# On-chip copy for half of KB, no ET transfers, shorter wa and kb loads, and Lu loaded in two parts

## The chip, the cores and the metric

The kernel runs on one core of a Trainium2 chip. The metric is device time: microseconds (us) from the start to the end of one execution. The profiler's record of one execution has a span (first to last instruction) that is a little shorter than that execution's own time.

## The reference

Three layers follow one another. The first is a recurrence over 768 time steps for 4 batches and 8 heads, 32 independent states of 40x40. Its output goes through a mixture of 8 experts with two chosen per token, and that through a dense feed-forward layer.

```python
def _attn_ref(r, k, v, w, a, b):
    state = np.zeros((B, H, D, D))
    for t in range(S):
        y[:, :, t] = np.einsum('bhd,bhde->bhe', rt, state)
        Sa = np.einsum('bhde,bhe->bhd', state, at)
        state_decay = state * wt[:, :, None, :] - np.einsum('bhd,bhe->bhde', Sa, bt)
        state = state_decay + np.einsum('bhd,bhe->bhde', vt, kt)
    return y
...
x = moe(x)                     # top 2 of 8 experts, relu(x @ w1[e]) @ w2[e]
h = x @ w_in
out = (h * tanh(softplus(h))) @ w_out
```

The change touches the recurrence alone, which is the class `Rec` of the kernel.

## The kernel before

The time steps are cut into 24 chunks of 32, and the 32 states into two halves of 16, so that the recurrence is a chain of 48 steps g: chunk g//2, half g%2. Inside a chunk the dependence between time steps is a triangular system of 32x32 for each state; it is solved for groups of 4 chunks at once on VectorE. Three generators run ahead of the chain and are interleaved with it by due times (`pump`): `prepare` (one chunk at a time), `solve` (one group of 4 chunks) and `apply` (one chunk).

`prepare` for a chunk i: VectorE scans the decays w (tile `wa`) to products `E` and reciprocals `R`; GpSimd multiplies `a` by `E` (`abd`, L235) and `k`, `b` by `R` (tile `kb`, L238); TensorE multiplies `abd` and `kb` (`pp`, L283), whose halves go to `Ls`, stored to the scratch `lscr` (L289), and into the tile `AM` (a part of `share`); TensorE transposes `kb` (L301), ScalarE copies it to `kn` (L307), and SyncE stores `kn` to a scratch `knd` in DRAM (L309); the transposed `E` becomes `EN` (L318). The first 40 columns of `AM` are `a` times `EN` (`scale_a`, L269): for that, SyncE loads `AT` and, by a second and a third transfer, moves the two halves of `EN` into the tile `ET`, because `EN` holds two chunks on its 128 partitions and `AM` one.

`solve` loads the four chunks' `lscr` into `Lu` (L411, 128 rows), works on VectorE (L439 to L454) and stores the result `Tt` to `tscr` (L488). `apply` loads `tscr` into the block-diagonal `Tbd` by four transfers (L386) and multiplies it with `AM` (L403) into `Zt`.

The chain at step g: `s_mm` (L561) multiplies the tile `KB` with the state `ST`, and VectorE scales that to the state two steps on (L566); `tr` transposes the state, `u_mm(g + 1)` (L548) gives the next step's rows, `y_mm(g - 1)` (L523) the output, with the right half of `KB` and `RR`; `rv_mm` (L593) fills `RR`. `KB[i % 2]` holds for chunk i, on partitions 64 to 127, the matrix `kn` twice, once for `s_mm` (x = 0) and once for `y_mm` (x = 1). One transfer from `knd` writes both (L496, a read that repeats each row), in the middle of every even step for the chunk after. It can't be issued until `y_mm` of the chunk before the present one has read the tile.

Every DMA named here is issued by SyncE in the order of the program, and each issue waits for what it needs before the next one is looked at. The DMAs take the completion counters DMAHW0 to DMAHW7 in turn, and an issue also waits for the DMA that had its counter before, the eighth one back.

Of the kernel before, what the change touches and what calls it, by code (L numbers as in the profile page):

```python
# [21 lines left out]
C = 32  # L22
NP = 2
# [9 lines left out]
LA = 2  # L33


def layout_rec(inp):

    c = np.ascontiguousarray

    def heads_t(x):  # L40
        return x.reshape(NP, PR, 2, NC, C, D).transpose(3, 2, 5, 1, 0, 4)


    wa = np.zeros((NC, 2, 64, NW + 1 + 2 * PR * C), np.float32)
    w33 = np.ones((NC, 2, 64, PR, 2, C + 1), np.float32)
    w33[..., 0] = 0
    w33[:, :, :D, :, :, 1:] = heads_t(inp["w"])
    wa[..., :NW] = w33.reshape(NC, 2, 64, NW)
    wa[:, :, :D, NW + 1:] = heads_t(inp["a"]).reshape(NC, 2, D, -1)
    at = inp["a"].reshape(NP, PR, 2, NC, C, D).transpose(3, 2, 0, 4, 1, 5)  # L50
    kb = np.zeros((NC, 2, 64, PR, 2, 2, C), np.float32)
    for x, n in enumerate("kb"):
        kb[:, :, :D, :, :, x] = heads_t(inp[n])
    rt = inp["r"].reshape(NP, HH, NC, C, D).transpose(2, 4, 0, 1, 3)
    vn = np.zeros((NC, NP, C, HH, 64), np.float32)
    vn[..., :D] = inp["v"].reshape(NP, HH, NC, C, D).transpose(2, 0, 3, 1, 4)
# [8 lines left out]
class Rec:  # L65


    def __init__(self, ctx, nc, tc, ins, emit_x, ident, share, late):
# [5 lines left out]
        self.pet = P("ret", 1)  # L74
# [9 lines left out]
        self.at = {}  # L84
# [5 lines left out]
    def consts_a(self):  # L90
# [110 lines left out]
    def pair(self, out, x, i, rows=RW):  # L201
        self.nc.sync.dma_start(out=out[0:rows], in_=self.ins[x][i, 0:rows])
# [48 lines left out]
    def load_at(self, i):  # L251

        t = self.last_x if i == 1 else [self.px.tile([128, HH // 2, D], F32, name="X") for _ in range(2)] if i == 2 else [
            self.pet.tile([128, PR, D], F32, name=n) for n in ("AT", "ET")]
        self.nc.sync.dma_start(out=t[0], in_=self.ins["at"][i].rearrange("p (a x) -> p a x", x=D))
        self.at[i] = t

    def load_et(self, i):

        en, et = self.EN[i // 2], self.at[i][1]  # L260
        r = 64 * (i % 2)
        for ab in range(2):
            self.nc.sync.dma_start(out=et[64 * ab:64 * ab + 64], in_=en[r:r + 64, ab])

    def scale_a(self, i):
        self.ready = i + 1
        if i in self.at:
            at, et = self.at.pop(i)
            self.nc.gpsimd.tensor_tensor(out=self.AM[i % (2 * GJ)][:, :, 0:D], in0=at, in1=et, op=ALU.mult)  # L269
# [55 lines left out]
    def prepare(self):  # L325
# [3 lines left out]
        for i in range(GJ, n):  # L329
            pos = iter([i / GJ - 2 + s / (6 * GJ) if i >= 2 * GJ else self.early(start[i - GJ][s]) for s in range(6)])  # L330
            if i == GJ:
# [24 lines left out]
            if i - LA >= GJ:  # L356
                self.scale_a(i - LA)
# [4 lines left out]
            if i == GJ:  # L362
                for x in range(2, GJ):
                    self.load_et(x)
                    self.scale_a(x)
            if i - LA + 1 >= GJ:
                self.load_at(i - LA + 1)
                self.load_et(i - LA + 1)
        for i in range(n - LA, n):
            yield (i + LA) / GJ - 2  # L370
            self.scale_a(i)
            if i + 1 < n:
                yield (i + LA + .5) / GJ - 2
                self.load_at(i + 1)
                self.load_et(i + 1)
# [230 lines left out]
    def chain(self, g, fill):  # L606
        if g == 0:
            self.u_mm(0)
        if g < NG - 2:
# [6 lines left out]
            if g % NP and OPT['kb'] == 1 and g > 1:  # L616
                self.load_kb(g // NP + 1)
# [12 lines left out]
        if g + 2 < NG:  # L630
# [6 lines left out]
            if g % NP == 0 and g and OPT['kb'] == 0:  # L637
                self.load_kb(g // NP + 1)
# [9 lines left out]
    def begin(self):  # L648
# [39 lines left out]
        for i in range(1, 3):  # L688
            self.load_at(i)
# [1049 lines left out]
```

## Time and profile before

| | us |
|---|---|
| median of 3 runs (1428.04 to 1430.09) | 1428.05 |
| profiled execution, own time | 1428.0 |
| its span | 1426.2 |
| busy in the span: PE | 1190.7 |
| DVE | 861.2 |
| ACT | 664.0 |
| POOL | 623.1 |

The profile names the engines PE (TensorE), DVE (VectorE), ACT (ScalarE), POOL (GpSimd) and SP (SyncE, which only issues DMAs here). The recurrence fills about the first 600 us. The first 124 us of it prepare the first chunks; there PE is busy a third of the time. In the rest PE is busy about four fifths of the time, at a mean granted clock of about 0.85 of full speed. The experts and the feed-forward layer fill the rest, where PE is nearly always busy. The chain of waits that ended last leads from the last instruction back through the feed-forward layer on PE and does not reach the recurrence, so that stage is read from its own waits.

### The profile page before, as it was taken

To read this page: it belongs to the slowest core of one execution; us is meant where nothing else is said; L and a number is where in the kernel's file an instruction comes from. 1 tells how busy PE (TensorE), PEld (TensorE's weight loads), DVE (VectorE), ACT (ScalarE), POOL (GpSimd) and SP (SyncE) were. 2 spreads that over 40 slices of the span, in tenths; PEclk is the share of its full clock that TensorE was granted. 3 is DMA by queue.
4 is the path that set the end of the run, shared out by engine and by line. 5 is a ranking of instruction groups with operands and counts; after the bars stand their busy time and mean duration, and the time that the engine had idled before them with its cause. 6 is when DMAs were issued, how large, how long until landed. Compare 5 with 4: busy or idle time off the path is not lost. (4 is left out here: it accounts for less than half of the span.)

```text
span 1426.2 us, 33947 instructions
## 1 busy us (share of the span) xinstructions
PE 1190.7 (83%) x13902; PEld 1135.5 (80%) x13902; DVE 861.2 (60%) x1570; ACT 664.0 (47%) x1419; POOL 623.1 (44%) x556
## 2 busy tenths in 40 slices
PE   3425778878787886885999999999888999999998
PEld 2325767767686775775999999998888999999998
DVE  8475837667493733362867876775236665556653
ACT  3423535545444433531443442442237666676664
POOL 4553734645262524162334544443045554454431
PEclk9557878988878888897999999999989999999999
DMA  6644667667755764424435545644245111110000
GB/s 152 156 132 129 162 152 193 177 149 182 178 132 114 127 111 85 141 77 133 128 104 179 163 148 179 204 142 148 66 114 155 29 36 32 29 47 10 15 15 20
DMA packets 147308, 165.64 MB, mean 116 GB/s; under 512 B 70294, under 2 KB 118422, under 8 KB 147126
## 3 DMA queue, kind: packets, MB, share of 16 engines
q1 hardware_dynamic: 136438, 140.85, 37.8%
q0 software_dynamic: 10688, 22.32, 5.8%
q8 instruction: 120, 1.97, 0.6%
q14 instruction: 62, 0.51, 0.1%
HBM read 116.06 MB, written 43.12 MB: 112 GB/s over the span
## 5 line engine op out<-in xcount | busy, mean ns | idle before, releaser
L1611 POOL TENSOR_TENSOR gl<-fh,gh 128x1024 fp32r<-128x1024 f32 x46 | 131.0, 2878 | 105.2 <-ACT gh L1627 101.9
L1253 PE MATMUL ph<-xh,w1h 128*128 128x256 f32 (+1 forms) x576 | 163.3, 296 | 12.0 <-issue 6.7
L1253 PE MATMUL ph<-xl,w1h 128*128 128x256 f32 (+1 forms) x576 | 162.5, 295 | 0.2
L1579 PE MATMUL fps<-fxh,ih 128*128 128x256 f32 x576 | 156.2, 286 | 1.4 <-DVE fh L1581 1.4
L1579 PE MATMUL fps<-fxl,ih 128*128 128x256 f32 x576 | 153.8, 281 | 0.5 <-DVE fxl L1109 0.3
L1610 DVE TENSOR_TENSOR fh<-fh,fp 128x1024 f32<-128x1024 f32 x48 | 95.0, 2014 | 60.3 <-ACT fp L1609 56.6
L1273 PE MATMUL py<-w2h,hh 128*128 128x320 f32 x400 | 129.2, 323 | 2.4 <-ACT hh L1105 1.6
L1107 DVE SCALAR_TENSOR_TENSOR hl<-ph,hh 128x512 fp32r<-128x512 f32 (+1 forms) x104 | 69.0, 665 | 103.0 <-ACT hh L1105 87.4
L1273 PE MATMUL py<-w2h,hl 128*128 128x320 f32 x400 | 125.7, 314 | 3.8 <-DVE hl L1107 3.6
L1273 PE MATMUL py<-w2l,hh 128*128 128x320 f32 x400 | 125.3, 313 | 2.0 <-DVE w2l L1109 2.0
L1253 PEld LDWEIGHTS ph<-xh,w1h 128*128 128x128 f32 x576 | 114.1, 198 | 13.3 <-issue 9.2
L1253 PEld LDWEIGHTS ph<-xl,w1h 128*128 128x128 f32 x576 | 114.3, 198 | 0.6 <-DVE xl L1109 0.6
L1641 PE MATMUL fpy<-oh,gl 128*128 128x320 f32 x384 | 114.6, 310 | 0.0
L1641 PE MATMUL fpy<-oh,gh 128*128 128x320 f32 x384 | 114.3, 310 | 0.0
L1641 PE MATMUL fpy<-ol,gh 128*128 128x320 f32 x384 | 113.9, 308 | 0.0
L1253 PE MATMUL ph<-xh,w1l 128*128 128x256 f32 (+1 forms) x384 | 112.9, 294 | 0.0
L1581 DVE COPY fh<-fps 128x512 f32<-128x512 f32 x96 | 64.6, 689 | 79.6 <-ACT fp L1580 73.7
L1579 PEld LDWEIGHTS fps<-fxh,ih 128*128 128x128 f32 x576 | 108.9, 189 | 1.8 <-DVE fh L1581 1.7
L1579 PEld LDWEIGHTS fps<-fxl,ih 128*128 128x128 f32 x576 | 109.0, 189 | 1.1 <-DVE fxl L1109 1.1
L1579 PE MATMUL fps<-fxh,il 128*128 128x256 f32 x384 | 107.7, 281 | 0.0
L1105 ACT ACTIVATE hh<-ph 128x512 fp32r<-128x512 f32 (+1 forms) x104 | 59.7, 580 | 98.7 <-PE ph L1253 91.8
L235 POOL TENSOR_TENSOR abd<-wa,E 40x512 f32<-40x512 f32 x40 | 64.4, 1609 | 66.7 <-issue 28.6
(276 smaller groups left out, 3306.4 us busy)
## 6 DMA issues: line engine op xcount, KB each, us to landing
KB<-knd SPq DMA_DIRECT2D x24, 640.0 KB
share<-in_w_dram SPq DMA_DIRECT2D x8, 1280.0 KB
wa<-in_wa_dram SPq DMA_DIRECT2D x22, 422.9 KB
kb<-in_kb_dram SPq DMA_DIRECT2D x20, 416.0 KB
share<-in_w_dram SPq DMA_DIRECT2D x8, 1024.0 KB
knd<-kn SPq DMA_DIRECT2D x24, 320.0 KB
yb<-y SPq DMA_DIRECT2D x22, 320.0 KB
ST<-in_vn_dram SPq DMA_DIRECT2D x48, 128.0 KB
```

Source lines behind the costliest of these rows:

```text
L235: (nc.vector if i <= OPT['nd'] else nc.gpsimd).tensor_tensor(out=abd[r, :, :, ab], in0=a[r], in1=E[r, :, :, 0:C], op=ALU.mult)
L1105: nc.scalar.activation(out=hi, in_=src, func=AF.Relu if relu else AF.Copy)
L1107: nc.vector.scalar_tensor_tensor(out=lo, in0=src, scalar=0.0, in1=hi.bitcast(F32), op0=ALU.max, op1=ALU.subtract)
L1253: nc.tensor.matmul(ph[:, m % c], lhsT=a, rhs=b, start=(q == 0), stop=(q == len(ops) - 1))
L1273: nc.tensor.matmul(py, lhsT=a[:, m, ts], rhs=b[:, m], start=(m == 0 and q == 0), stop=(m == FC - 1 and q == 2))
L1579: nc.tensor.matmul(ph[:, i], lhsT=a, rhs=b, start=(q == 0), stop=(q == len(ops) - 1))
L1581: nc.vector.tensor_copy(h[:, 2 * m2:2 * m2 + 2], ph)
L1610: mul = lambda s: nc.vector.tensor_tensor(out=h[:, s], in0=h[:, s], in1=p[:, s], op=ALU.mult)
L1611: low = lambda s: (nc.vector if last and s.start % 8 else nc.gpsimd).tensor_tensor(out=gl[:, s], in0=h[:, s], in1=gh[:, s].bitcast(F32), o ...
L1641: nc.tensor.matmul(py, lhsT=a[:, m, ts], rhs=w[:, m], start=(q == 0), stop=(q == len(ops) - 1))
```

## The change

`KB`: the transfer from `knd` writes the x = 0 half alone (320 KB in place of 640 KB), and a new `copy_kb` on ScalarE copies it, one step's part at a time, to the x = 1 half, behind the state copies of `u_mm`. The load is issued in odd steps, behind `u_mm`, for two chunks on. It waits for `s_mm` and `copy_kb` of the same step.

`ET`: the tile and its two transfers per chunk are gone. `AT` has one fixed tile, whose partitions 0 to 63 and 64 to 127 take even and odd chunks like `EN`, and `scale_a` multiplies `AT` and `EN` by two operations on 64 partitions, which write across to `AM`. It stands at the end of each chunk's `prepare`, no longer two chunks later, and issues the `AT` load of two chunks on.

Padding: from chunk 4 on, `wa` and `kb` are loaded by two transfers of 40 rows each, without the 24 rows between.

`Lu`: loaded in two parts, 96 rows for the first three chunks of the group, and 32 rows for the last.

```diff
-    at = inp["a"].reshape(NP, PR, 2, NC, C, D).transpose(3, 2, 0, 4, 1, 5)
+    at = inp["a"].reshape(NP, PR, 2, NC, C, D).transpose(3, 0, 4, 2, 1, 5)
...
     def pair(self, out, x, i, rows=RW):
-        self.nc.sync.dma_start(out=out[0:rows], in_=self.ins[x][i, 0:rows])
+
+        for r in (slice(0, rows),) if i < GJ else (slice(0, D), slice(64, RW)):
+            self.nc.sync.dma_start(out=out[r], in_=self.ins[x][i, r])
...
     def load_at(self, i):
-        t = self.last_x if i == 1 else [...] if i == 2 else [
-            self.pet.tile([128, PR, D], F32, name=n) for n in ("AT", "ET")]
-        self.nc.sync.dma_start(out=t[0], in_=self.ins["at"][i].rearrange("p (a x) -> p a x", x=D))
-        self.at[i] = t
-
-    def load_et(self, i):
-
-        en, et = self.EN[i // 2], self.at[i][1]
-        r = 64 * (i % 2)
+        if i < len(self.seq):
+            r = 64 * (i % 2)
+            self.nc.sync.dma_start(out=self.AT[r:r + 64].rearrange("p b a x -> p (b a x)"), in_=self.ins["at"][i])
+
+    def scale_a(self, i):
+
+        self.ready = i + 1
+        en, r = self.EN[i // 2], slice(64 * (i % 2), 64 * (i % 2) + 64)
         for ab in range(2):
-            self.nc.sync.dma_start(out=et[64 * ab:64 * ab + 64], in_=en[r:r + 64, ab])
-
-    def scale_a(self, i):
-        self.ready = i + 1
-        if i in self.at:
-            at, et = self.at.pop(i)
-            self.nc.gpsimd.tensor_tensor(out=self.AM[i % (2 * GJ)][:, :, 0:D], in0=at, in1=et, op=ALU.mult)
+            self.nc.gpsimd.tensor_tensor(out=self.AM[i % (2 * GJ)][64 * ab:64 * ab + 64, :, 0:D], in0=self.AT[r, ab], in1=en[r, ab], op=ALU.mult)
+        self.load_at(i + 2)
...
-    def load_l(self, k):
-        self.nc.sync.dma_start(out=self.Lu[:, 0:C * C], in_=self.lscr[k].rearrange("u q t i -> (u q) (t i)"))
+    def load_l(self, k, j0=0, j1=GJ):
+        self.nc.sync.dma_start(out=self.Lu[32 * j0:32 * j1, 0:C * C],
+                               in_=self.lscr[k][PR * j0:PR * j1].rearrange("u q t i -> (u q) (t i)"))
...
         if k:
+
+            self.wants[1] = lambda: self.made < GJ * (k + 1) - 1
+            yield s0 - .2
+            self.load_l(k, 0, GJ - 1)
             self.wants[1] = lambda: self.made < GJ * (k + 1)
             yield s0 - OPT["ll"]
-            self.load_l(k)
+            self.load_l(k, GJ - 1)
...
     def load_kb(self, i):
+
         KB, kn = self.KB[i % 2], self.KN.pop(i)
-        self.nc.sync.dma_start(out=KB.rearrange("p c x h d -> p x (c h d)")[64:128], in_=kn[:, None].to_broadcast([64, 2, 2 * HH * D]))
+        self.nc.sync.dma_start(out=KB[64:128, :, 0].rearrange("p c h d -> p c (h d)"), in_=kn.rearrange("p (c x) -> p c x", c=2))
+
+    def copy_kb(self, g):
+        t = self.KB[(g // NP) % 2][64:128, g % NP]
+        self.nc.scalar.copy(out=t[:, 1], in_=t[:, 0])
...
         if g + 1 < NG:
             self.u_mm(g + 1)
+        self.copy_kb(g)
+        if g % NP and g // NP + 2 < NC:
+            self.load_kb(g // NP + 2)
...
-            if g % NP == 0 and g and OPT['kb'] == 0:
-                self.load_kb(g // NP + 1)
```

On SyncE, in the middle of the recurrence, one chunk's transfers behind its `knd` stand so before (the names in brackets are what an issue waits for; a counter DMAHWn stands for the DMA that used it last):

```order
L496 DMA KB_140<-knd 64x2x1280 [waits DMAHW5_49,PE_49]
L309 DMA knd<-kn 2x64x640 [waits DMAHW6_49,Activation_49]
L501 DMA ST_422<-in_vn_dram 32x1024 [waits DMAHW7_49]
L506 DMA RR_424<-in_rt_dram 40x1024 [waits DMAHW0_49]
L386 DMA Tbd_190<-tscr 32x8x32 [waits DMAHW1_49]
L386 DMA Tbd_190<-tscr 32x8x32 [waits DMAHW2_49]
L386 DMA Tbd_190<-tscr 32x8x32 [waits DMAHW3_49]
L386 DMA Tbd_190<-tscr 32x8x32 [waits DMAHW4_49]
L255 DMA AT<-in_at_dram 128x320 [waits DMAHW5_49,Pool_49]
L263 DMA ET<-EN 64x320 [waits DMAHW6_49]
L263 DMA ET<-EN 64x320 [waits DMAHW7_49]
```

The `KB` load stood just ahead of `knd`, and the first `ET` was the one that waited for `knd`'s counter, DMAHW6. The same place of the changed kernel, on SyncE, from `knd` on:

```order
L303 DMA knd<-kn 2x64x640 [waits DMAHW5_49,Activation_49]
L486 DMA ST_422<-in_vn_dram 32x1024 [waits DMAHW6_49,PE_49]
L491 DMA RR_424<-in_rt_dram 40x1024 [waits DMAHW7_49,PE_49]
L361 DMA Tbd_188<-tscr 32x8x32 [waits DMAHW0_49]
L361 DMA Tbd_188<-tscr 32x8x32 [waits DMAHW1_49]
L361 DMA Tbd_188<-tscr 32x8x32 [waits DMAHW2_49]
L361 DMA Tbd_188<-tscr 32x8x32 [waits DMAHW3_49]
L255 DMA AT<-in_at_dram 64x640 [waits DMAHW4_49,Pool_49]
L477 DMA KB_138<-knd 64x1280 [waits DMAHW5_49,PE_49,Activation_49]
L386 DMA Lu<-lscr 32x1024 [waits DMAHW6_49]
```

`KB` now stands eight behind `knd`, so it is the one that waits for `knd`'s counter, and it loads a chunk that is needed a step and a half later than before.

On SyncE, before the chain starts, the first group's solution `tscr` is stored behind the seventh `knd`:

```order
L289 DMA lscr<-Ls 128x8x32 [waits DMAHW5_49,Activation_49]
L202 DMA kb_146<-in_kb_dram 104x1024 [waits DMAHW6_49,PE_49]
L309 DMA knd<-kn 2x64x640 [waits DMAHW7_49,Activation_49]
L488 DMA tscr<-Tt 128x1024 [waits DMAHW0_49,DVE_49]
L255 DMA AT<-in_at_dram 128x320 [waits DMAHW1_49,Pool_49]
L263 DMA ET<-EN 64x320 [waits DMAHW3_49,DMAHW2_49]
L263 DMA ET<-EN 64x320
L202 DMA wa_142<-in_wa_dram 104x1041 [waits DMAHW4_49,DVE_49,Pool_49]
L386 DMA Tbd_189<-tscr 32x8x32 [waits DMAHW5_49,DMAHW0_49]
```

The same place on SyncE in the changed kernel:

```order
L283 DMA lscr<-Ls 128x8x32 [waits DMAHW0_49,Activation_49]
L202 DMA kb_143<-in_kb_dram 40x1024 [waits DMAHW1_49,PE_49]
L202 DMA kb_143<-in_kb_dram 40x1024 [waits DMAHW2_49]
L468 DMA tscr<-Tt 128x1024 [waits DMAHW3_49,DVE_49]
L386 DMA Lu<-lscr 96x1024 [waits DMAHW4_49,DMAHW0_49]
L303 DMA knd<-kn 2x64x640 [waits DMAHW5_49,Activation_49]
L361 DMA Tbd_187<-tscr 32x8x32 [waits DMAHW6_49,DMAHW3_49]
```

`tscr` is now ahead of that `knd`, and neither an `AT`, an `ET` nor a `wa` stands between it and the `Tbd` load that reads it.

On GpSimd at the start of the recurrence the operations stand so before (`share<-AT,ET` and its like with `lx` and `X`, which served as `AT` and `ET` for chunks 1 and 2, are `scale_a`):

```order
L293 TENSOR_TENSOR share<-share,mml 128x8x32 x4
L269 TENSOR_TENSOR share<-AT,ET 128x8x40
L235 TENSOR_TENSOR abd_162<-wa_142,E 40x16x32 x2
L238 TENSOR_TENSOR kb_145<-kb_145,R 104x1024
L133 MEMSET share 128x16x24
L235 TENSOR_TENSOR abd_166<-wa_143,E 40x16x32 x2
L238 TENSOR_TENSOR kb_146<-kb_146,R 104x1024
L269 TENSOR_TENSOR share<-lx_110,lx_111 128x8x40
L293 TENSOR_TENSOR share<-share,mml 128x8x32
L269 TENSOR_TENSOR share<-X 128x8x40
L269 TENSOR_TENSOR share<-AT,ET 128x8x40
L235 TENSOR_TENSOR abd_162<-wa_142,E 40x16x32 x2
```

In the changed kernel GpSimd has there:

```order
L287 TENSOR_TENSOR share<-share,mml 128x8x32 x4
L262 TENSOR_TENSOR share<-AT,EN 64x8x40 x6
L235 TENSOR_TENSOR abd_160<-wa_139,E 40x16x32 x2
L238 TENSOR_TENSOR kb_142<-kb_142,R 104x1024
L262 TENSOR_TENSOR share<-AT,EN 64x8x40 x2
L131 MEMSET share 128x16x24
L235 TENSOR_TENSOR abd_164<-wa_140,E 40x16x32 x2
L238 TENSOR_TENSOR kb_143<-kb_143,R 104x1024
L287 TENSOR_TENSOR share<-share,mml 128x8x32
L262 TENSOR_TENSOR share<-AT,EN 64x8x40 x2
L235 TENSOR_TENSOR abd_160<-wa_139,E 40x16x32 x2
```

Three of the four `scale_a` moved ahead of the first `abd`; none of them waits for a transfer of `EN` any more.

## Rows read from the trace of the kernel before

**Rows 1.** Waits, whole run: engine, line, releaser; us in total, times, longest us.

```profile
DVE tm L439 <- DMA Lu<-lscr: 62.6, 6, 18.3
POOL share L269 <- DMA ET<-EN: 58.0, 12, 17.0
PE cs L561 <- DMA KB<-knd: 43.3, 12, 6.3
```

**Rows 2.** Busy us (and instructions) of PE, PEld, DVE, ACT, POOL; clock, DMA share, GB/s.

```profile
205.00:405.00 200.00, 156.09 (x3281) 141.74 (x3282) 132.12 (x209) 99.08 (x294) 94.60 (x62) 0.85 0.69 171
```

**Rows 3.** The tile KB from 205 to 405 us: its loads and who waited.

```profile
L496 SPq DMA_DIRECT2D KB<-knd x11: 632/637/1881, 201.0 to 403.9; - x11
...
  PE cs L561: 31.9, 10
```

**Rows 4.** Timeline of PE, s_mm alone: start, length, instruction, idle before and releaser.

```profile
331.92 1.30 PE L561 MATMUL cs<-ST,KB 128*40 128x40 f32 x32 [4.43 <-DMA KB<-knd]
...
350.20 0.81 PE L561 MATMUL cs<-ST,KB 128*40 128x40 f32 x32 [2.31 <-DMA KB<-knd]
```

**Rows 5.** Timeline of SP's DMA issues, from one KB load to the next.

```profile
321.91 0.64 SPq L496 DMA_DIRECT2D KB<-knd  x1
322.64 0.55 SPq L309 DMA_DIRECT2D knd<-kn  x1
...
332.80 1.55 SPq L255 DMA_DIRECT2D AT<-in_at_dram  x1
336.46 1.14 SPq L263 DMA_DIRECT2D ET<-EN  x2
...
339.11 0.31 SPq L202 DMA_DIRECT2D wa<-in_wa_dram  x1
...
339.97 2.12 SPq L202 DMA_DIRECT2D kb<-in_kb_dram  x1
342.18 0.64 SPq L496 DMA_DIRECT2D KB<-knd  x1
342.90 0.56 SPq L309 DMA_DIRECT2D knd<-kn  x1
```

**Rows 6.** DMA issues by tile: count and KB each.

```profile
KB<-knd SPq DMA_DIRECT2D x24, 640.0 KB
...
wa<-in_wa_dram SPq DMA_DIRECT2D x22, 422.9 KB
kb<-in_kb_dram SPq DMA_DIRECT2D x20, 416.0 KB
...
knd<-kn SPq DMA_DIRECT2D x24, 320.0 KB
```

**Rows 7.** Timeline: the first knd store, and the ACT copy that waits for it.

```profile
34.51 0.64 SPq L309 DMA_DIRECT2D knd<-kn  x1
...
43.76 0.75 ACT L307 COPY kn<-pp 128x320 f32<-128x320 f32 x2 [3.35 <-DMA knd<-kn]
```

**Rows 8.** Timeline of DVE, POOL, PE and SP before the chain starts.

```profile
71.97 1.26 DVE L224 TENSOR_TENSOR_SCAN E<-wa,d 104x528 f32<-104x528 f32 x1 [10.60 <-DMA wa<-in_wa_dram]
...
89.94 1.43 POOL L269 TENSOR_TENSOR share<-X 128x320 f32<-128x320 f32 x1 [9.08 <-DMA X<-EN]
...
93.79 2.33 DVE L454 TENSOR_REDUCE Tt<-tm 128x64 f32<-128x1024 f32 x2
...
98.40 1.94 PE L283 MATMUL pp<-kb,abd 104*32 104x64 f32 x64 [18.10 <-POOL kb L238]
...
103.60 1.48 SPq L488 DMA_DIRECT2D tscr<-Tt  x1
...
118.50 1.78 PE L403 MATMUL pp<-Tbd,share 128*96 128x128 f32 x7 [12.01 <-DMA Tbd<-tscr]
```

**Rows 9.** Groups by line: count, busy us, mean ns of one, idle before.

```profile
L269 POOL TENSOR_TENSOR share<-AT,ET 128x320 f32<-128x320 f32 x22 | 24.8, 1126 | 69.8 <-DMA ET<-EN 58.0 <-DVE d1b L227 6.7 <-DVE Tt L441 5.1
...
L169 ACT ACTIVATE KB<-ident 40x640 f32<-40x640 f32 x4 | 2.8, 732 | 0.1
```

More of the change, by code (lines that the diff above doesn't have):

```diff
@@ L32 @@
 RW = 64 + D
-LA = 2
 def layout_rec(inp):
@@ L58, in layout_rec @@
     rows = lambda x: c(flat(x)[:, :64 + D])
-    return dict(wa=rows(wa), at=flat(c(at)), kb=flat(kb), r=c(heads_t(inp["r"])).reshape(NC, 2, D, -1), rt=c(rt).reshape(NC, D, -1), vn=vn)
+    return dict(wa=rows(wa), at=c(at).reshape(NC, 64, -1), kb=flat(kb), r=c(heads_t(inp["r"])).reshape(NC, 2, D, -1), rt=c(rt).reshape(NC, D, -1), vn=vn)
 UR = (96, 32)
@@ L73, in __init__ @@
         self.p2, self.px = P("r2", 2), P("rx", 3)
-        self.pet = P("ret", 1)
         self.pen = P("ren", 6)
@@ L83, in __init__ @@
         self.scaled, self.lscr, self.tscr, self.Ec = {}, {}, {}, {}
-        self.at = {}
         self.KN, self.ZT, self.EN, self.WE = {}, {}, {}, {}
@@ L103, in consts_a @@
         self.kb3 = self.share[:, 6 * PR * 96:6 * PR * 96 + 4 * PR * C].rearrange("p (a b s c) -> p a b s c", a=PR, b=2, s=2)
+        self.AT = one.tile([128, 2, PR, D], F32, name="AT")
         for i in range(GJ):
@@ L251, in load_at @@
     def load_at(self, i):
-        t = self.last_x if i == 1 else [self.px.tile([128, HH // 2, D], F32, name="X") for _ in range(2)] if i == 2 else [
-            self.pet.tile([128, PR, D], F32, name=n) for n in ("AT", "ET")]
-        self.nc.sync.dma_start(out=t[0], in_=self.ins["at"][i].rearrange("p (a x) -> p a x", x=D))
-        self.at[i] = t
-    def load_et(self, i):
-        en, et = self.EN[i // 2], self.at[i][1]
-        r = 64 * (i % 2)
-        for ab in range(2):
-            self.nc.sync.dma_start(out=et[64 * ab:64 * ab + 64], in_=en[r:r + 64, ab])
+        if i < len(self.seq):
+            r = 64 * (i % 2)
+            self.nc.sync.dma_start(out=self.AT[r:r + 64].rearrange("p b a x -> p (b a x)"), in_=self.ins["at"][i])
     def scale_a(self, i):
         self.ready = i + 1
-        if i in self.at:
-            at, et = self.at.pop(i)
-            self.nc.gpsimd.tensor_tensor(out=self.AM[i % (2 * GJ)][:, :, 0:D], in0=at, in1=et, op=ALU.mult)
+        en, r = self.EN[i // 2], slice(64 * (i % 2), 64 * (i % 2) + 64)
+        for ab in range(2):
+            self.nc.gpsimd.tensor_tensor(out=self.AM[i % (2 * GJ)][64 * ab:64 * ab + 64, :, 0:D], in0=self.AT[r, ab], in1=en[r, ab], op=ALU.mult)
+        self.load_at(i + 2)
     def prods(self, i):
@@ L337, in prepare @@
                     pass
+                self.scale_a(GJ - 1)
                 self.gaps(6, 2)
@@ L344, in prepare @@
                 next(sc)
-            if i == GJ:
-                self.load_et(1)
-                self.load_at(3)
             yield next(pos)
             next(sc, None)
-            if i == GJ:
-                self.scale_a(1)
             if i + 1 < n:
@@ L355, in prepare @@
             self.mask(i)
-            if i - LA >= GJ:
-                self.scale_a(i - LA)
             if i + 2 < n:
@@ L361, in prepare @@
                 yield next(pos)
[L362 to L370, printed above, removed]
             self.scale_a(i)
[L372 to L375, printed above, removed]
     def solve(self):
@@ L615, in chain @@
                 self.load_r(g // NP + 1)
-            if g % NP and OPT['kb'] == 1 and g > 1:
-                self.load_kb(g // NP + 1)
             self.s_mm(g)
@@ L636, in chain @@
                 self.load_rbd(g // NP + 1)
-            if g % NP == 0 and g and OPT['kb'] == 0:
-                self.load_kb(g // NP + 1)
         fill()
@@ L662, in begin @@
         self.setup()
+        for i in range(2):
+            self.load_at(i)
         for i in range(GJ):
@@ L669, in begin @@
                 pass
+            self.scale_a(i)
             if i == 0:
-                self.load_at(0)
-                self.load_et(0)
-                self.scale_a(0)
                 self.load_v(0)
@@ L687, in begin @@
                 self.load_kb(1)
-        for i in range(1, 3):
-            self.load_at(i)
     def run(self):
```

## The prediction

> **What bounds the kernel now.** I read the page first: the chain that ended last lies in the feed-forward layer, so it says nothing of the recurrence, and everything behind the recurrence simply starts when it ends. I then read the waits by engine. Three of them are on transfers that the change touches: PE on `KB`, 43.3 us in 12 waits, POOL on `ET`, 58.0 us, DVE on `Lu`, 62.6 us in 6 [rows 1]. Only the first is PE's own; the other two matter as far as PE or SP later waits for these engines.
>
> The third view is busy time by stretch. From 205 to 405 us PE is busy 156.09 of 200 us; no other engine is nearer to full [rows 2]. In that stretch PE waits 31.9 us for `KB` in 10 waits, and the loads come every (403.9 - 201.0) / 10 = 20.3 us, once per chunk [rows 3]. Each wait is the tail of a transfer: the load issued at 321.91 is in use at 331.92, the one issued at 342.18 at 350.20, 10 and 8 us later [rows 4, 5].
>
> Why is the load issued so late? SP's own timeline answers it. Between the `knd` store at 322.64 and the first `ET` at 336.46, eight issues later, SP gets through seven issues in 13.8 us; from there to the next `knd` it takes 6.4 us [rows 5]. The eighth issue behind a DMA waits for that DMA's counter, so 13.8 us is the time that `knd` takes to land. The chunk's cycle of 20.26 us (322.64 to 342.90) is `knd`'s landing plus the rest of the issues [rows 5]. So SP, in its fixed order, sets the pace, and PE feels it as the wait on `KB`.
>
> `knd` is a store of 320 KB that takes longer than the 640 KB of `KB` [rows 5, 6]. The Trainium skill, "DMA: Bandwidth & Descriptors", section "Why a DMA increments its semaphore by 16 and not by 1", says that a DMA runs on as many engines (at most 16) as divide the outermost sizes of both sides; `knd`'s outermost size is 2, so by it two engines carry the store, and the trace's durations agree.
>
> **The change part by part.** *KB earlier.* The load of a chunk moves from the middle of the even step ahead of its chunk to the odd step before that, about a step earlier in the program (half a cycle, 10 us [rows 5]), against waits of 3.2 us in the mean (31.9 / 10) [rows 3]. In SP's order it now waits for `knd`, which holds it until up to 13.8 us behind that store [rows 5], but two steps of work still lie between. So I take the direct wait as gone. What is late next is SP's cycle itself, and it is this that limits the gain.
>
> *SP's cycle after.* With little ahead of it `knd` landed in at most 43.76 - 34.51 = 9.25 us [rows 7]; in the cycle above it took 4.6 us more [rows 5]. Directly ahead of it stand `wa`, `kb` and `KB`, 423 + 416 + 640 KB [rows 6]; the last is 43% of that, 2.0 of the 4.6 us, and it now stands behind. That leaves 11.8 us. The other issues took 6.44 us; the `ET` pair's 1.24 us (336.46 to the next issue, 1.14 us long and a gap of 0.1) goes, and a second `wa` (0.31 us [rows 5]) and a second `kb`, which I put at the same, come with their gaps, 0.8 us. So 11.8 + 6.0 = 17.8 us. PE's own floor without the `KB` waits is (200 - 31.9) / 200 x 20.3 = 17.1 us [rows 2, 3]. The larger counts: 17.8 us, a saving of 2.4 us per cycle. Ends: 19.8 us if `knd` still takes 13.8, 17.1 us if SP no longer matters. Ten cycles between 205 and 405 us: 24 us. The 11.4 us of `KB` waits outside that stretch (43.3 - 31.9) [rows 1, 3] shrink by the same share, 2.4 of 3.2: 9 us.
>
> *Padding.* The rows taken out are (422.9 - 325) + (416 - 320) = 194 KB a chunk [rows 6], an estimate from 40 of 52 rows. By share of bytes they would cut the 4.6 us of queueing by 194 / 1479, 0.6 us a cycle. I take 0, since the two transfers in place of one cost issue time already counted, and keep 0 to 0.6 x 12 = 7 us for the range.
>
> By the rule named above this edit gives less than its bytes: 104 rows run on 13 engines with 8 rows each, 40 rows on 10 engines with 4 each, and two such transfers put 8 rows on the same ten again. The engines that `knd` uses would carry as much as before. By the rule the sum is 1384, by the bytes 1377; no row here shows engines one by one.
>
> *Before the chain starts.* The first group's solve ends at 93.79 + 2.33 = 96.1 us, but `tscr` is stored at 103.60, because SP stands at a `knd` ahead of it, which needs products that PE made only at 98.40, after 18.1 us of waiting for POOL [rows 8]. POOL had waited for `EN` transfers, 9.08 us at 89.94 alone [rows 8]. These transfers go, and `tscr` no longer stands behind that `knd`: 7.5 us. The solve had itself lost 10.60 us at 71.97 behind a `wa` load [rows 8], queued behind two `KB` loads that are now half as large; I take 4 us of it. Together 11.5 us, of the range 0 (if PE's 12.01 us for `Tbd` [rows 8] only begins earlier and grows) to 7.5 + 10.6 = 18 us.
>
> *Lu.* Its six waits sit on DVE, 10.4 us each [rows 1]. The last part is loaded at the same place as before, only smaller, and SP's lateness is in it. I take 0; up to 10.4 x 5 / 4 = 13 us if a quarter of the rows lands in a quarter less and PE follows, and not below 0, since the last part is never issued later than the whole was.
>
> *Added work.* 48 copies on ACT of 640 elements per partition, 732 ns each as the nearest row has it: 35 us [rows 9]. ACT is busy 99 of 200 us [rows 2], and each copy stands behind the state copies that PE waits for; its readers are the `Y` product a step later and the next `KB` load. I take 0; 35 us if all lay on the path. POOL does two operations for one, of 64 partitions with the same 320 elements each; the trace has none on 64, so between 0 and 22 x 1.126 = 25 us more [rows 9], and I take 25, by elements per partition. POOL is busy 94.6 of 200 us and gets back 58 us of waits [rows 1, 2], so on the path 0.
>
> Sum: 24 + 9 + 11.5 = 44 us, from the profiled execution's own 1428.0 us (span 1426.2, 1.8 outside): 1384 us. The median of the runs, 1428.05, is the same within a tenth.
>
> **The rivals.** *`knd` still sets the pace.* `KB`'s place in the queue is taken by other loads, `knd` lands in 13.8 us, the cycle is 19.8 and saves 0.44 us twelve times, and of the start only the 7.5 us come: 1428 - 5 - 7.5 = 1415 us. For it: `knd` itself is untouched. Against: the clean 9.25 us [rows 7].
>
> *PE runs free.* All 43.3 us go, 18 us at the start, and PE, no longer stopped, keeps its fast clock: `s_mm` took 1.30 us behind a wait of 4.43 us and 0.81 behind 2.31 [rows 4], 0.5 us for each of 12 waits, 6 in all. 1428 - 67 = 1361 us. Against: SP's floor above PE's.
>
> *Slower: SP stops at `AT`.* `scale_a` now stands at the end of its own chunk, behind the `EN` copies, and the `AT` load behind it stops SP until POOL is done; the `KB`, `wa`, `lscr` and state loads are queued behind. `AT` was issued 10.2 us behind `knd` [rows 5], and up to 13.8 us it costs nothing, as `KB` waits for `knd` anyway. From 13.8 + 2.4 us it takes more than the change gives. If POOL, held by its two extra operations and the solve's products, were done 17.7 us behind `knd`, the cycle would be 1.5 us longer than the old one: over some 14 cycles, and less the 7.5 us at the start, 1428 + 21 - 7.5 = 1441 us. For it: two chunks of slack are given away. Against: POOL is half idle [rows 2].
>
> *Nothing moves.* The wait on `KB` turns into waits on DVE, which has 132 of 200 us of work [rows 2] and 10 us of `Lu` in a group of four cycles: 1428 us. Against: 132.12 / 200 of four cycles of 20.3 us are 54 us, and 54 + 10 of 81 leave it room down to cycles of 16 us.
>
> **How the numbers follow.** Forecast 0.63, `knd`'s pace 0.18, PE free 0.08, slower 0.07, nothing 0.04. A measurement of this kernel tells 0.2%, 2.9 us, from no change. Faster: 0.63 + 0.18 + 0.08 = 0.89, less 0.01 for a `knd` case with the start given back: 0.88; same 0.05; slower 0.07. The range reaches to both neighbours: 1360 to 1417, which leaves out the slower and the unmoved case and the edges, under 0.2.
>
> **What would show it.** Right: no wait of PE on `KB`; `KB` loads every 17 to 18.5 us; eight issues from `knd` to `KB` in about 12 us; `tscr` first stored near 92 to 97 us, and the chain begun some 11 us earlier; no wait of POOL on a transfer of `EN`; the ACT copies with no PE wait behind them. Wrong: `knd` to `KB` still 13.8 us or more, SP waiting for POOL at `AT`, or PE's idle time back under the names of DVE, `Tbd` or the `ST` loads.

## The result, and the profile after

The changed kernel takes 1388.37 us (median of 4 runs, 1383.63 to 1395.27). The kernel before took 1428.05 us beside it (4 runs, 1425.68 to 1430.09). The ratio is 0.9726, with a 95% interval of 0.968 to 0.9773; a second measurement on another chip gave 0.9724 (0.9692 to 0.9757). The forecast was 1384 us. The profiled execution was the slowest of the four, 1395.27 us with a span of 1393.5 us and a mean granted clock of 0.917.

The longest waits of PE from 100 to 553 us, which holds the whole recurrence of the changed kernel (engine, tile, line and releaser; us in total, times, longest us):

```profile
PE pp L378 <- DMA Tbd<-tscr: 21.7, 5, 14.6
PE cs L533 <- issue: 11.8, 12, 1.8
PE cs L533 <- DMA ST<-in_vn_dram: 10.4, 4, 2.9
PE cs L533 <- DVE RR L589: 9.5, 6, 2.7
```

No row is left of the 43.3 us of `KB` [rows 1]. What stands there is short, but for one wait on `Tbd` of 14.6 us ahead of the first step. Part of the freed time came back: the waits on `Tbd`, on the `ST` load and on `RR` were 27.8 us in the recurrence of the kernel before (100 to 600 us), and are 41.6 now. Before:

```profile
PE pp L403 <- DMA Tbd<-tscr: 12.0, 1, 12.0
...
PE cs L548 <- DMA ST<-in_vn_dram: 8.7, 4, 4.3
PE cs L548 <- DVE RR L604: 7.1, 4, 3.3
```

DVE's wait on `Lu` has shrunk to 43.6 us from the 62.6 us of [rows 1]:

```profile
DVE tm L419 <- DMA Lu<-lscr: 43.6, 6, 13.7
```

Busy us and instruction counts from 205 to 405 us, columns as in [rows 2]:

```profile
205.00:405.00 200.00, 166.09 (x3603) 149.72 (x3604) 154.16 (x239) 120.06 (x336) 122.14 (x79) 0.89 0.50 137
```

PE is busy for 10 us more, and every engine executes more instructions in the same 200 us. POOL is busy 122 us where it was 95, and the DMA engines are half idle. The granted clock is 0.89 where it was 0.85 [rows 2], and PE's busy time for one matmul is 46.1 ns (166.09 / 3603) where it was 47.6 (156.09 / 3281). At 3281 matmuls that is, as an estimate, 5 us, which the prediction's sum did not have.

Where in the program did the time come from? The first product with `KB` in a step (`s_mm`) is a good ruler, since each of the steps 0 to 45 has it. Steps 0, 8, 28 and 44 in the kernel before, from the timeline of PE (start, length, instruction, idle before and releaser):

```profile
124.19 0.27 PE L561 MATMUL cs<-ST,KB 128*40 128x40 f32 x2 [0.51 <-ACT ST L551]
...
209.49 0.76 PE L561 MATMUL cs<-ST,KB 128*40 128x40 f32 x16 [5.03 <-DMA KB<-knd]
...
417.95 0.81 PE L561 MATMUL cs<-ST,KB 128*40 128x40 f32 x32
...
552.10 0.50 PE L561 MATMUL cs<-ST,KB 128*40 128x40 f32 x14
```

The same four steps after:

```profile
117.87 0.27 PE L546 MATMUL cs<-ST,KB 128*40 128x40 f32 x2 [0.51 <-ACT ST L536]
...
192.08 0.78 PE L546 MATMUL cs<-ST,KB 128*40 128x40 f32 x32
...
382.81 0.81 PE L546 MATMUL cs<-ST,KB 128*40 128x40 f32 x32
...
513.38 0.51 PE L546 MATMUL cs<-ST,KB 128*40 128x40 f32 x16
```

The chain starts 6.3 us earlier. Steps 0 to 8 give 11.1 us, the ten cycles from step 8 to 28 give 17.7 (208.46 to 190.73 us), and steps 28 to 44 give 3.6: 38.7 us in all. The spans differ by only 32.7 us (1426.2 less 1393.5). The other 6 us were lost behind step 44 in this one execution; in the second profile of the changed kernel step 44 starts at 513.90 us and the span is 1388.2 us, so there all 38 us are kept.

SP's queue over one cycle, after, from one `KB` load to the next:

```profile
307.23 0.53 SPq L477 DMA_DIRECT2D KB<-knd  x1
...
308.48 0.68 SPq L497 DMA_DIRECT2D rbd<-in_r_dram  x2
312.35 1.54 SPq L202 DMA_DIRECT2D wa<-in_wa_dram  x2
...
315.40 0.55 SPq L303 DMA_DIRECT2D knd<-kn  x1
...
323.25 0.49 SPq L255 DMA_DIRECT2D AT<-in_at_dram  x1
323.84 0.70 SPq L477 DMA_DIRECT2D KB<-knd  x1
```

And all `KB` loads in that stretch (count, issue length min/median/max in ns, first and last start in us):

```profile
L477 SPq DMA_DIRECT2D KB<-knd x11: 444/451/697, 213.3 to 404.7; - x11
```

The loads come every (404.7 - 213.3) / 10 = 19.1 us, where it was 20.3 [rows 3]. The load is now issued 8.4 us behind `knd`; in eleven cycles this distance lies between 8.4 and 11.7 us. It is not always `knd` that holds it. SP's waits from 205 to 405 us (line and releaser; us in total, times, longest us) are:

```profile
SPq L255 <- POOL share L262: 17.6, 5, 4.2
SPq L303 <- ACT kn L301: 17.0, 4, 7.2
...
SPq L477 <- DMA knd<-kn: 11.4, 5, 2.6
```

So the `KB` load waits for `knd` in five of the eleven cycles. In the cycle shown it does not: there SP stands 3.3 us at `AT` for POOL.

The way up to the chain, from the timelines of DVE, PE and SP:

```profile
70.94 1.26 DVE L224 TENSOR_TENSOR_SCAN E<-wa,d 104x528 f32<-104x528 f32 x1 [13.83 <-DMA wa<-in_wa_dram]
...
83.92 1.93 PE L277 MATMUL pp<-kb,abd 104*32 104x64 f32 x64 [4.91 <-POOL kb L238]
95.14 1.94 PE L277 MATMUL pp<-kb,abd 104*32 104x64 f32 x64 [5.85 <-POOL kb L238]
...
96.77 2.33 DVE L434 TENSOR_REDUCE Tt<-tm 128x64 f32<-128x1024 f32 x2
...
99.13 0.36 SPq L468 DMA_DIRECT2D tscr<-Tt  x1
...
111.72 3.70 PE L378 MATMUL pp<-Tbd,share 128*96 128x128 f32 x16 [14.64 <-DMA Tbd<-tscr]
```

Against [rows 8]: PE's 18.10 us behind POOL have become 4.91 and 5.85, and `tscr` is stored 4.5 us sooner, right when the solve ends (96.77 + 2.33 = 99.10 us). But the solve itself ends 3.0 us later than before. DVE's wait on `wa` has grown from 10.60 to 13.83 us, so that the scan behind it starts only 1.0 us sooner; from there to the end of the solve DVE takes 28.2 us where it took 24.2, and no run shows why. PE's wait on `Tbd` has grown from 12.01 to 14.64 us.

### The profile page after: what moved, and what is told of

The parts are those of the page before. It is cut to its first block, busy times and chain, and to the rows that moved or that the text cites. A ratio compares the mean times of both kernels' runs of the same rounds, so it can differ in the third digit from the quotient of the medians.

```text
span 1393.5 us, 34124 instructions
## 1 busy us (share of the span) xinstructions
PE 1180.4 (85%) x13902; PEld 1124.5 (81%) x13902; DVE 856.3 (61%) x1570; ACT 698.5 (50%) x1467; POOL 656.2 (47%) x580
## 5 line engine op out<-in xcount | busy, mean ns | idle before, releaser
L1235 PEld LDWEIGHTS ph<-xh,w1h 128*128 128x128 f32 x576 | 113.5, 197 | 11.6 <-issue 7.6
L589 DVE TENSOR_TENSOR RR<-cs,mrv 64x256 f32<-64x256 f32 x96 | 40.6, 423 | 96.7 <-PE cs L578 78.6
```

What stands on the lines that cost most here:

```text
L589: nc.vector.tensor_tensor(out=ro, in0=rvv, in1=self.mrv[r, None, :].to_broadcast([64, 8, C]), op=ALU.mult)
L1235: nc.tensor.matmul(ph[:, m % c], lhsT=a, rhs=b, start=(q == 0), stop=(q == len(ops) - 1))
```

## Experiments

The theory to be tested: SP issues in order, an issue waits for the DMA eight places back, and the slow `knd` store therefore sets the pace of SP and the lateness of `KB`. The rivals put the gain elsewhere (the `ET` pair, the bytes), or the loss (POOL at `AT`, the copies on ACT).

The chips differ: the kernel before took 1429.14, 1407.52 and 1427.31 us in the three sets. So ratios to it are compared, not times; an expectation in microseconds is read against the ratio times 1428.

**Each part alone.** The first, `KB`, in its core:

```diff
-        self.nc.sync.dma_start(out=KB.rearrange("p c x h d -> p x (c h d)")[64:128], in_=kn[:, None].to_broadcast([64, 2, 2 * HH * D]))
+        self.nc.sync.dma_start(out=KB[64:128, :, 0].rearrange("p c h d -> p c (h d)"), in_=kn.rearrange("p (c x) -> p c x", c=2))
...
+        self.copy_kb(g)
+        if g % NP and g // NP + 2 < NC:
+            self.load_kb(g // NP + 2)
```

> The kernel before with the first part alone: half of KB loaded and copied on ScalarE, the load issued in the odd step. Theory (SP issues in order, knd's landing paces it, KB's lateness is what PE feels): PE's wait on KB goes, knd lands about 2 us sooner because the 640 KB ahead of it are gone, so some 12 cycles are 2 us shorter, about 1404 us (1395 to 1412). Rival 1 (the ET pair and the start carry the gain): KB's wait is replaced by another, 1420 us or more. Rival 2 (the copies on ScalarE cost time on the path): a part of 35 us is lost, 1428 us or more.

Measured: 1406.11 us, ratio 0.9837 (0.9799 to 0.9875), as the theory has it. PE has no wait on `KB` any more, and step 44 starts 27.4 us before that of the kernel before (524.75 against 552.10). DVE's wait on `wa` ahead of the chain is shorter by 3.4 us than in [rows 8]:

```profile
68.39 1.26 DVE L224 TENSOR_TENSOR_SCAN E<-wa,d 104x528 f32<-104x528 f32 x1 [7.21 <-DMA wa<-in_wa_dram]
```

The second, `ET`:

```diff
-            self.nc.sync.dma_start(out=et[64 * ab:64 * ab + 64], in_=en[r:r + 64, ab])
...
+            self.nc.gpsimd.tensor_tensor(out=self.AM[i % (2 * GJ)][64 * ab:64 * ab + 64, :, 0:D], in0=self.AT[r, ab], in1=en[r, ab], op=ALU.mult)
+        self.load_at(i + 2)
```

> The kernel before with the second part alone: no ET transfers, POOL multiplies from EN in two halves, AT loaded two chunks ahead. Theory: the start gives 6 to 8 us and the two issues saved give about 1.2 us in each cycle, but KB stays late behind the SP queue and PE's wait on it stays: 1406 to 1420 us. Rival 1 (this part carries the gain): 1400 us or less. Rival 2 (SP stops at AT until POOL is done, and the KB load, which here stands behind AT, comes later than before): 1432 us or more, PE's waits on KB above 43 us.

Measured: 1423.46 us, ratio 0.9947 (0.9904 to 0.999), a little less than expected (0.9947 x 1428 = 1420). The first step starts at 126.23 us, 2 us later than before and not 6 to 8 earlier: alone this part does not bring the start forward. DVE's wait on `wa` is 14.94 us there, and its scan starts at 74.45 us. PE's waits on `KB` are 27.3 us.

The third, the padding:

```diff
-        self.nc.sync.dma_start(out=out[0:rows], in_=self.ins[x][i, 0:rows])
+        for r in (slice(0, rows),) if i < GJ else (slice(0, D), slice(64, RW)):
+            self.nc.sync.dma_start(out=out[r], in_=self.ins[x][i, r])
```

> The kernel before with the third part alone: the loads of wa and kb from chunk 4 on in two transfers of 40 rows each, no padding. Theory: nothing by bytes, and two more issues in SP's order of about 0.4 us each with knd's wait now standing two issues earlier: between 1426 and 1434 us. Rival (the bytes ahead of knd count): 194 KB less a chunk bring 0.6 us or more a cycle, 1420 us or less.

Measured: 1435.12 us, ratio 1.0045 (0.9999 to 1.009). The bytes bring nothing by themselves; whether the part costs something alone, the interval leaves just open.

The fourth, `Lu`:

```diff
+            yield s0 - .2
+            self.load_l(k, 0, GJ - 1)
             self.wants[1] = lambda: self.made < GJ * (k + 1)
             yield s0 - OPT["ll"]
-            self.load_l(k)
+            self.load_l(k, GJ - 1)
```

> The kernel before with the fourth part alone: Lu loaded in two parts, the last quarter by itself. Theory: the last quarter is issued at the same place of SP's order as the whole was, so DVE's wait on Lu loses little and PE gains nothing: 1425 to 1430 us. Rival: the quarter lands in a quarter of the time, DVE's 62.6 us fall to 15 to 30 us and PE follows: 1415 us or less.

Measured: 1431.43 us, ratio 1.0022 (0.9986 to 1.0057): nothing. DVE's wait on `Lu` is 60.0 us, hardly less than the 62.6 before. So the parts one by one come to -1.63 - 0.53 + 0.45 + 0.22 = -1.5%, and the whole to -2.7%. The profiles show where the surplus lies. At the first step (120.32, 126.23, 126.90 and 125.09 us against 124.19) the parts one by one add up to a loss of 1.8 us, and the whole gains 6.3, in its second profile 8.2. From there to step 44 they add up to 27.0 us, and the whole gains 32.4 and 30.0.

**The knd store, with nothing of the change.** The test on which the theory stands or falls:

```diff
-        (nc.scalar if i < OPT['dk'] else nc.sync).dma_start(out=self.KN[i].rearrange("r (c x) -> c r x", c=2), in_=kn.rearrange("p h d -> p (h d)"))
+        for c in range(2):
+            nc.sync.dma_start(out=self.KN[i][:, c * HH * D:c * HH * D + HH * D], in_=kn[64 * c:64 * c + 64].rearrange("p h d -> p (h d)"))
```

> The kernel before, with nothing of the change, but the knd store split into two stores of 64 rows each (one per half chunk, same bytes, same destination), so that the outermost size of each is 64 and not 2. Theory (knd's slow landing paces SP and so KB): the landing falls from 12 to 14 us to 9 or less, SP's cycle from 20.3 us toward PE's floor of 17 to 18, PE's waits on KB to under 15 us, and the time to 1400 to 1413 us with no other edit. Rival (KB is late because of bytes or because of what SP waits for elsewhere): knd is not what counts, 1423 us or more, waits on KB stay near 43 us.

Measured: 1353.61 us beside 1407.52, ratio 0.961 (0.9573 to 0.9647). That is more than the whole change brings, and more than was expected (0.961 x 1428 = 1372). Waits of PE from 100 to 553 us, the loads of `KB`, and the first step in this kernel:

```profile
PE cs L562 <- DMA KB<-knd: 16.9, 8, 6.2
```

```profile
L497 SPq DMA_DIRECT2D KB<-knd x12: 623/624/986, 205.3 to 408.0; - x12
```

```profile
100.98 0.27 PE L562 MATMUL cs<-ST,KB 128*40 128x40 f32 x2 [0.51 <-ACT ST L552]
```

The same `KB` load of 640 KB, at its old place, makes PE wait for 16.9 us and not 43.3, and the cycle is (408.0 - 205.3) / 11 = 18.4 us. That is the theory's part. But the first step starts at 100.98 us and not at 124.19: 23.2 us of the gain lie ahead of the chain, where PE does not wait for `KB` at all.

**The knd store in the changed kernel.** The same edit, there:

```diff
+        for c in range(2):
+            nc.sync.dma_start(out=self.KN[i][:, c * HH * D:c * HH * D + HH * D], in_=kn[64 * c:64 * c + 64].rearrange("p h d -> p (h d)"))
```

> The changed kernel with the knd store split into two stores of 64 rows each. Theory (knd still sets part of SP's cycle of 19.15 us, PE's floor is 17.1): SP's waits on knd, some 24 us in all, go; PE follows for a part of it: 1370 to 1383 us. Rival (with KB early PE is held by its own neighbours, the state copies, RR and Tbd, and SP has slack): 1385 to 1391 us, the cycle stays at 19 us.

Measured: 1345.31 us beside 1407.52, ratio 0.9551 (0.9521 to 0.9582), better than expected again. But two stores also have two places in the queue. To tell that from the shape, `knd` was laid out in memory so that one store has 128 rows on both sides:

```diff
-        self.KN[i] = self.pkn.tile([64, 2 * HH * D], F32, name="knd")
-        (nc.scalar if i < OPT['dk'] else nc.sync).dma_start(out=self.KN[i].rearrange("r (c x) -> c r x", c=2), in_=kn.rearrange("p h d -> p (h d)"))
+        self.KN[i] = self.pkn.tile([128, HH * D], F32, name="knd")
+        (nc.scalar if i < OPT['dk'] else nc.sync).dma_start(out=self.KN[i], in_=kn.rearrange("p h d -> p (h d)"))
...
-in_=kn.rearrange("p (c x) -> p c x", c=2))
+in_=kn.rearrange("(c p) x -> p c x", c=2))
```

> The changed kernel with knd kept as 128 rows of 640 (half chunk outermost) in memory, so that its store is one transfer with an outermost size of 128 on both sides and not 2; the same bytes, the same 2560-byte rows, the same number of issues. Theory (the outermost size of 2 is what made knd slow): as with knd split into two stores, a ratio of 0.950 to 0.958 to the kernel before. Rival (the split helped because two transfers have two counters, or start one after the other): the ratio stays at 0.966 or more, and KB still waits 8 to 12 us behind knd.

Measured: 1361.80 us beside 1427.31, ratio 0.955 (0.9516 to 0.9583), the same as with two stores. So it is the shape and not the number of transfers. (The `KB` load here reads two runs of 2560 bytes a row in place of one of 5120; with two stores it was unchanged.) The clean case of [rows 7] shows the landing. In the changed kernel, from SP's and ACT's timelines:

```profile
35.44 0.61 SPq L303 DMA_DIRECT2D knd<-kn  x1
...
45.23 0.75 ACT L301 COPY kn<-pp 128x320 f32<-128x320 f32 x2 [4.62 <-DMA knd<-kn]
```

and with the 128-row store:

```profile
35.21 0.43 SPq L303 DMA_DIRECT2D knd<-kn  x1
...
40.28 0.74 ACT L301 COPY kn<-pp 128x320 f32<-128x320 f32 x2
```

ACT may overwrite `kn` once the store has landed: 9.8 us behind the issue in the one, and at most 5.1 us in the other, where it does not wait at all. The rule that the prediction cites from the Trainium skill, "DMA: Bandwidth & Descriptors", section "Why a DMA increments its semaphore by 16 and not by 1", agrees: an outermost size of 2 gives two engines, 128 gives sixteen. No row names the engines, but the trace holds the time of every count that a transfer adds to its completion counter, and these counts fit. Behind a first count at 1.03 us, the `knd` issued at 35.44 us adds two, at 9.60 and 9.70 us; the 128-row store adds sixteen, between 4.05 and 4.67 us. By the last count `knd`, from 200 to 410 us, lands 13.2 us behind its issue in the mean of eleven before (10.3 to 15.1), 10.2 after (9.1 to 11.6), and 4.1 with 128 rows (2.4 to 6.0).

The same counts show a second cost of the store, beside the order of SP's issues. In the changed kernel the `wa` load issued at 56.99 us stands behind a `knd` whose two counts come at 63.94 and 65.49 us. Behind a first one that comes at once, that load adds ten counts: eight within 3.81 us of its issue, the last two at 10.34 and 12.96. Before, it is eleven of thirteen within 8.21 us, and the last two at 14.44 and 14.82. With the 128-row store all ten come between 6.14 and 7.28 us. So two parts of a load behind the old store come late, as they would on two engines that the store still holds, and the load has landed only with them.

What SP itself loses to the store is in its waits up to 540 us (line and releaser; us in total, times, longest us). The kernel before:

```profile
SPq L263 <- DMA knd<-kn: 32.4, 12, 4.9
...
SPq L501 <- DMA knd<-kn: 9.5, 2, 5.1
...
SPq L386 <- DMA knd<-kn: 7.9, 2, 4.3
```

after:

```profile
SPq L477 <- ACT KB L481: 32.1, 7, 11.1
SPq L255 <- POOL share L262: 31.2, 10, 6.2
...
SPq L202 <- POOL abd L235: 16.9, 13, 3.9
...
SPq L477 <- DMA knd<-kn: 15.4, 7, 2.6
SPq L361 <- DMA knd<-kn: 9.0, 2, 4.8
...
SPq L303 <- DMA knd<-kn: 6.5, 1, 6.5
```

and with the 128-row store:

```profile
SPq L255 <- POOL share L262: 55.7, 16, 6.3
...
SPq L477 <- DMA knd<-kn: 0.8, 2, 0.4
```

From the rows shown that is 50 us before and 31 after; with the new layout 0.8 us and one wait of 0.6 are left, and SP stops for POOL instead. Of the 32.1 us for ACT's copy after, 31.0 lie behind 405 us; there SP is up with the chain, as the copy belongs to the step that PE is at. `wa` gains as well: DVE's 13.83 us behind it ahead of the chain are not there any more, and the first step starts at 104.53 us. The same scan with the 128-row store:

```profile
60.34 1.26 DVE L224 TENSOR_TENSOR_SCAN E<-wa,d 104x528 f32<-104x528 f32 x1 [2.29 <-ACT EN L312]
```

**SP's stop at AT.** The load of the next chunk's `AT` one chunk later, when POOL is long past the buffer:

```diff
-        self.load_at(i + 2)
+        if i:
+            self.load_at(i + 1)
```

> The changed kernel with the AT load of a chunk issued one chunk later, so that the POOL product that frees its buffer is long past and SP no longer stops for POOL there (31.2 us in 10 stops). Theory (the stop at AT delays the KB load and the loads behind it, but KB has two steps of slack): SP's waits move to the next issue, the time is 1383 to 1391 us. Rival (POOL's product at the end of the chunk is the next pacer): 10 us or more come, 1379 us or less.

Measured: 1372.72 us beside 1407.52, ratio 0.9747 (0.9706 to 0.9787), no different from the change as it is (0.9726). The stop has left `AT` and come back elsewhere, as SP's waits up to 540 us in this kernel show:

```profile
SPq L202 <- POOL abd L235: 42.5, 19, 6.2
...
SPq L478 <- DMA knd<-kn: 21.0, 9, 3.1
```

The wait for `knd` at the `KB` load grew from 15.4 to 21.0 us: part of the time that SP had stood at `AT` was time in which `knd` was not there yet anyway. More of it is found at the `wa` and `kb` loads (L202), where SP's wait for POOL grew from 16.9 to 42.5 us. So this stop by itself costs nothing; what SP's waits for POOL cost in all is not shown, since this run did not take them away.

**The change without its padding part:**

```diff
-        for r in (slice(0, rows),) if i < GJ else (slice(0, D), slice(64, RW)):
-            self.nc.sync.dma_start(out=out[r], in_=self.ins[x][i, r])
+        self.nc.sync.dma_start(out=out[0:rows], in_=self.ins[x][i, 0:rows])
```

> The changed kernel without its third part: the loads of wa and kb whole, with padding rows, one issue each. Theory (the padding's bytes give nothing and the two more issues cost): 1380 to 1388 us, so the part costs up to 6 us, as it did alone. Rival (with KB's bytes gone the padding is what stands ahead of knd, so leaving it out pays): 1394 us or more.

Measured: 1382.80 us beside 1407.52, ratio 0.9809 (0.9774 to 0.9843), the rival's side. The whole change had 0.9726 and 0.9724, on other chips, so inside the change this part is worth about 0.8%, with intervals that lie close to each other (one ends at 0.9773, the other begins at 0.9774). By the start of step 44 it is 8 us (521.44 against 513.38 and 513.90), 0.6%.

**The change without its KB part,** `load_kb` and its place as in the kernel before:

```diff
-        self.copy_kb(g)
-        if g % NP and g // NP + 2 < NC:
-            self.load_kb(g // NP + 2)
...
+            if g % NP == 0 and g and OPT['kb'] == 0:
+                self.load_kb(g // NP + 1)
```

> The changed kernel without its first part: KB whole, loaded late as before; the other three parts stay. Theory (KB's lateness is what PE feels, and the other parts only pay once it is gone): the three parts together are worth about what they are one by one, +2 us, so a ratio of 0.993 to 1.005 to the kernel before, and PE's waits on KB stay above 25 us. Rival (the 13 us by which the whole change beats the sum of its parts come from the other three together): a ratio of 0.986 or less.

Measured, on the chip of the next run: 1412.21 us, ratio 0.9882 (0.9838 to 0.9926), between the two. PE's waits on `KB` over the whole run:

```profile
PE cs L541 <- DMA KB<-knd: 28.3, 11, 4.8
```

So they stay, as the theory had it, but the other three parts together bring 1.2% where one by one they add up to nothing. Which two of them do that was not tried.

**The change again, and with doubled copies.**

> The changed kernel once more, beside the three below on the same chip, since the kernel before has differed by about 20 us between chips: a ratio of 0.968 to 0.977 to the kernel before, as measured first, if the ratio carries from chip to chip; a ratio outside of it if it doesn't, and then the single runs are compared with this one alone.

Measured: 1387.94 us beside 1427.31, ratio 0.9724 (0.9692 to 0.9757); the ratio carries from chip to chip.

```diff
-        self.nc.scalar.copy(out=t[:, 1], in_=t[:, 0])
+        for _ in range(2):
+            self.nc.scalar.copy(out=t[:, 1], in_=t[:, 0])
```

> The changed kernel with each of the 48 copies of the KB half on ScalarE made twice: 48 x 0.72 = 35 us more of ScalarE work. Theory (the copies are hidden behind TensorE, as the prediction's sum has it): 0 to 8 us slower than the changed kernel. Rival (they stand on the path, between the state copies that TensorE waits for, and hold back the next KB load): 20 to 35 us slower, and then the change's own copies cost as much.

Measured: 1396.51 us, ratio 0.9786 (0.9745 to 0.9827): 8.6 us above the change on the same chip by the medians, just beyond the theory's range and far from the rival's, with overlapping intervals. In the profiled executions the step 44 starts at 514.94 us against 513.90, and the spans are 1389.3 and 1388.2 us. So 35 us of copies cost between 1 and 9 us.

## Why the prediction was right, and where its steps were not

- *KB's direct wait goes:* right, no such wait is left, and this part alone brings 1.6% of the 2.7%.
- *SP's cycle, 17.8 us:* 19.1 us. The two halves were off in opposite ways. `knd` landed in 10.2 us in the mean where 11.8 was taken. The share by bytes was not what failed: with the KB part alone `knd` lands in 11.3 us in the mean, 1.9 sooner than the 13.2 before, where the sum took 2.0. But the 13.8 that it started from was one cycle, and the padding, taken at 0, gives about the 0.6 us a cycle that its bytes gave (10.8 us without that part). The rest of the cycle was put at 6.0 us, issues alone; in the cycle shown it is 8.2 us from `KB` to `knd` (307.23 to 315.40), of which SP stands 3.2 us ahead of `wa`. From 205 to 405 us SP waits 17.6 us for POOL's two products and 17.0 for ACT's `kn`, neither of which the sum had.
- *The sum of the recurrence, 24 + 9 = 33 us:* 32.4 us from step 0 to step 44 (38.7 less 6.3). The ten cycles gave 17.7 and not 24; the rest of the recurrence gave 14.7 and not 9, most of it in the first eight steps, 11.1 us. The sum held by luck: one error covered the other.
- *The start, 11.5 us:* 6.3, in the second profile 8.2 (124.19 to 115.96). Two terms made it up. The queue's 7.5 us came in full, since `tscr` is stored as soon as the solve ends; but the solve ended 3.0 us later, so `tscr` came at 99.13 and not at 92 to 97. The 4 us of `wa` is the term that failed. It was put down to two `KB` loads in the queue, and for most of the load that was right: eleven of thirteen counts came within 8.21 us before, eight of ten within 3.81 after. But a load is there only with its last two parts, and these came behind the `knd` store: at 69.95 us, and at 70.82 for the second transfer of `wa`, where the whole had come at 71.85. The KB part alone does bring 3.6 us at this scan (71.97 to 68.39), and the ET part alone takes 2.5 (74.45); in the whole 1.0 is left. With the 128-row `knd` store the scan starts at 60.34.
- *Padding, 0:* alone it costs 0.45%, 6 us, or nothing, on the other side of the 0 to 7 us that were kept for it; inside the change it gives 0.6 to 0.8%, 8 to 12 us, at or above the most that the sum by bytes had. One number for both places does not exist.
- *Lu, 0:* right. The 19 us by which DVE's wait on `Lu` shrank are hardly this part's, which alone leaves 60.0 of 62.6 us; with the ET part alone they are 47.7.
- *Copies on ACT, 0, and POOL, 0 on the path:* for the copies nearly right; twice as many cost 1 to 9 us. POOL's two products take 1114 ns each, on 64 partitions, as long as one on 128 did (1126 [rows 9]); so the 25 us more were right. That they cost nothing on the path is not shown.
- *Signs of being wrong:* PE's idle time did come back in part under the names of `Tbd`, the `ST` loads and DVE, 13.8 us (41.6 less 27.8) against the 43.3 that went, and SP does wait for POOL at `AT`.
- *The rival "`knd` still sets the pace"* was wrong in its time (1415 us) and in part right in its mechanism: the `KB` load waits for `knd` in five of eleven cycles, and the loads ahead of the chain land behind it. `knd` does still cost the changed kernel about 1.8% (0.9726 to 0.955), 25 us. *PE runs free* (1361 us) is near what the kernel comes to with that gone: 0.955 x 1428 = 1364 us. *SP stops at `AT`* happens, 31.2 us in all, and taking this stop away brings nothing.

The store was named as the pacer, and its cost was then taken as given, since the change did not touch it. It is the one thing that was worth most: the kernel before with its store in two pieces alone beats the change (0.961 against 0.9726), and with it the change's four parts are worth only 0.9551 / 0.961, 0.6%.

What stays open: why the parts give more together than alone, most of it ahead of the first step, and which of them work on each other.

## What to carry over

When a queue that issues in order paces a kernel, look for the transfer that lands slowest for its bytes, and at the outermost size on both of its sides, before moving the loads behind it. A store of 320 KB that was held up by an outermost size of 2 cost more than all the late loads, padding and extra transfers around it. It cost twice: the queue stood until it landed, and loads issued behind it had their last parts land late. And an edit priced alone can have the other sign beside others that share its queue: it is best priced in the kernel in which it will stand.

## What the runs showed of the hardware

In ten of the fourteen profiles, those of the kernel before and after among them, the step from 44 to 45 takes some 25 us, with all engines but POOL nearly standing still. In the four of the chip on which the kernel before took 1407.52 us it takes 4 to 5 us. The busy times of PE, PEld, DVE, ACT and POOL of the changed kernel in that stretch:

```profile
514.00:535.00 21.00, 6.58 (x49) 4.05 (x50) 1.25 (x3) 0.46 (x3) 14.54 (x27) 0.56 0.20 37
```

The change without its padding part, on that other chip, in the same steps:

```profile
521.44 0.81 PE L544 MATMUL cs<-ST,KB 128*40 128x40 f32 x32
...
525.56 0.89 PE L544 MATMUL cs<-ST,KB 128*40 128x40 f32 x32
```

POOL issues its indirect loads of `ids` in both. What stops the other engines was not found. The 20 us are as large as the difference between the chips; so the kernel before, which has no trace on that chip, probably lacks the stop there too, and each ratio then has it on both sides or on neither.
